# In the first two blocks the activation stays in PSUM and VectorE makes its low part; four units' attention weights are scaled on ScalarE

## Chip, cores and metric

The kernel runs on one core of one Trainium2 chip, as one program. The metric is the device time of that core in microseconds (us). Engines are named as the profile names them: PE is TensorE (PEld its weight loads), DVE is VectorE, ACT is ScalarE, POOL is GpSimd, SP is SyncE, which here issues most of the DMAs.

## What is computed

Three layers follow each other. First comes windowed attention over 4 batches of 8 heads of 576 positions (half of the heads see the last 32 positions, half every fourth of the last 128); then a dense layer; then a layer of eight experts, of which each token takes two.

```
attn = exp(scores - max);  attn = attn / (sum(attn) + 1e-9);  y = attn @ v
h = x @ w_in                      # 2304 x 512 times 512 x 2048
g = h * cos(h)
x1 = g @ w_out                    # 2304 x 2048 times 2048 x 512
top-2 of 8 experts per token;  out += weight * (relu(x1 @ w1[e]) @ w2[e])
```

All of it is fp32 in and out. Matrix products of the dense layer and the experts are made of three passes in a narrower format: each operand is split in a high part and a low part (the operand less its high part), and high x high, high x low and low x high are summed.

## The kernel before

Attention works on 16 *units* (two heads of one batch each). For a unit, `a_scores` makes the scores in PSUM and their row maxima, `a_exp` makes nine ACTIVATEs (one for each of nine pieces of 64 rows per head, with the running sums read out behind each), `a_norm` multiplies the nine pieces with the reciprocal of their sums, and `a_part` transposes the pieces (lines 507 and 510) and multiplies with v (line 527, copied out by lines 535 and 544). Units 0 to 7 take the fused exponential just told; units 0 to 3 are done in an opening ahead of the loop.

The dense layer works on blocks of 256 tokens and on pairs `p` of 0 to 7 of 256 hidden columns. A *step* is one block and one pair. The first 16 steps alternate between blocks 0 and 1 (step i is pair i // 2 of block i % 2), because in this stretch the weights of the layer arrive by DMA and are cut: each 512-column piece of a pair's weights takes three VectorE instructions (`w_bits`, lines 312 to 314), then ScalarE makes the high part (line 320) and GpSimd the low part (line 321, `w_parts`). From step 16 on the weights lie ready and block after block runs through the eight pairs.

In a step TensorE makes `ph` (`g1`, line 584). Then `post` makes h * (sin²(h/2) − 0.5), which is −h * cos(h) / 2: ScalarE rounds h / 2π to an integer (line 592), VectorE takes the remainder (line 593), ScalarE takes the sine and the square (lines 595 and 596), VectorE multiplies with `ph` (line 597), ScalarE makes the high part of g (line 600) and GpSimd the low part (line 601). Two steps later TensorE uses g (`g2`, line 611). `ph` has two buffers in PSUM, and so have r and g in SBUF: the `ph` of step i is used again in step i + 2, as soon as its readers have ended.

What stands beside a step, and where in it, is told by a table (`BESIDE`, one line for each place): pieces of weights, attention of later units, splits of x for later blocks. Each engine runs its instructions in the order in which the program is written, so what waits on an engine holds up all that stands behind it. The scaling of unit 4 stands in step 0, of unit 5 ahead of step 5, of unit 6 in step 8, of unit 7 ahead of step 12. `x_split` of block 2 (line 570) stands at the end of step 14 and in step 15, and step 16 needs it.

Of the kernel before, what the change touches and what calls it, by code (L numbers as in the profile page):

```python
# [9 lines left out]
F32 = mybir.dt.float32  # L10
# [4 lines left out]
AF = mybir.ActivationFunctionType  # L15
ALU = mybir.AluOpType
# [4 lines left out]
NB = 9  # L21
# [21 lines left out]
FUSED = 8  # L43
# [186 lines left out]
def kernel(ctx: ExitStack, tc: tile.TileContext, qT, kT, v, wm, we, wg, noise, out):  # L230
    nc = tc.nc
# [254 lines left out]
    def a_norm(u):  # L486
        s = U[u][2]
        if u in SM:
            sm = SM.pop(u)
        else:  # L490
            sm = small.tile([P, NB], F32, tag="sm", name=f"sm{u}", bufs=3)
            nc.vector.tensor_reduce(sm, s, axis=AX.X, op=ALU.add)
        nc.vector.tensor_scalar(sm, sm, 1e-9, None, op0=ALU.add)
        nc.vector.reciprocal(sm, sm)
        for i in range(0, NB, 3):
            nc.gpsimd.tensor_tensor(s[:, i:i + 3], s[:, i:i + 3],
                                    sm[:, i:i + 3, None].to_broadcast([P, 3, KW]), op=ALU.mult)
# [76 lines left out]
    def g1(blk, p, cs=range(4)):  # L574
        t, w = XHL[blk], WM[p]
        if (blk, p) not in PH:
            tag, bufs = ("acc", 4) if (blk, p) == (0, 1) else ("ph", 2)
            PH[blk, p] = psum.tile([P, 2, TB], F32, tag=tag, name=f"ph{blk}_{p}", bufs=bufs)
        ph = PH[blk, p]
        for j in range(2):  # L580
            for c in cs:
                for n, (a, x) in enumerate(PASSES):
                    o = c * 256 + j * P
                    nc.tensor.matmul(ph[:, j, :], w[:, a, o:o + P], t[:, x, c, :],  # L584
                                     start=(c == 0 and n == 0 and (j == 0 or len(cs) == 4)), stop=(c == 3 and n == 2),
                                     skip_group_check=(len(cs) < 4))
        return ph.rearrange("p a b -> p (a b)")

    def post(blk, p, ph):
        r = bpool.tile([P, 512], F32, tag="r", name=f"r{blk}_{p}", bufs=2)  # L590
        n = r.bitcast(I32)
        nc.scalar.activation(n, ph, AF.Copy, scale=1.0 / TWO_PI)  # L592
        nc.vector.scalar_tensor_tensor(r, n, -TWO_PI, ph, op0=ALU.mult, op1=ALU.add)  # L593
        yield
        nc.scalar.activation(r, r, AF.Sin, scale=0.5)  # L595
        nc.scalar.activation(r, r, AF.Square)  # L596
        nc.vector.scalar_tensor_tensor(r, r, 0.5, ph, op0=ALU.subtract, op1=ALU.mult)  # L597
        yield
        g = bpool.tile([P, 2, 512], F32R, tag="g", name=f"g{blk}_{p}", bufs=2)
        nc.scalar.activation(g[:, 0, :], r, AF.Copy)  # L600
        nc.gpsimd.tensor_tensor(g[:, 1, :], r, g[:, 0, :].bitcast(F32), op=ALU.subtract)  # L601
        G[blk, p] = g

    def g2(blk, p, ts=range(2)):
# [133 lines left out]
    def r_send(blk, t):  # L738
        si, pay = RT[blk]
        for k in range(2):  # L740
# [6 lines left out]
            if blk >= NBLK - 2:  # L747
                tc.declare_no_dep(d.ins, EARLY[0].ins, reason="expert 0's first slots are final")
            scat.append(d)


    ops.update(S=a_scores, E=a_exp, N=a_norm,
               T=lambda u, c, eng="": a_trans(u, c, eng == "a"),
               A=lambda u, g, eng="": a_av(u, g, eng == "a"),
# [17 lines left out]
    for u in range(4, FUSED):  # L772
        at_step(START[u - 4] + 2, -1, a_norm, u)
        at_step(START[u - 4] + 3, 0 if u == 4 else -1, a_part, u, 0)
    pieces = [(0, 2), (0, 3)] + [(j, k) for j in range(1, NPAIR) for k in range(4) if (j, k) > (1, 1)]
    for n, (j, k) in enumerate(pieces):
        i = n // 2
# [8 lines left out]
    for u in range(4, 16):  # L786
        i = START[u - 4]
        if i > 0:
            at_step(i, 2, a_scores, u)
        if i > 0:  # L790
            at_step(i + 1, 2, a_exp, u)
        if u >= FUSED:
            at_step(i + 2, 1, a_norm, u)
        if u >= FUSED:
            at_step(i + 3, 0, a_part, u, 0)
        at_step(i + 3, 2, a_part, u, 1)
        at_step(i + 4, 0, a_part, u, 2)
        if u + 1 < 16:
            at_step(max(i + 1, 0), 0, a_loadqk, u + 1)
            at_step(i + 4, 2, a_loadv, u + 1)  # L800
# [203 lines left out]
    for line in BESIDE.split("\n"):  # L1004
        at, *names = line.split() or ("",)
        for n in names:
            i, pos = map(int, at.split(":"))
# [4 lines left out]
    for i, (blk, p) in enumerate(steps):  # L1012
        if i == 48:
            actx.close()
            c1 = ctx.enter_context(tc.tile_pool(name="c1", bufs=1, side="right"))
        ph = g1(blk, p, range(3, 4) if i < 2 else range(4))
        run(i, -1)
        po = post(blk, p, ph)
        next(po)
        if i >= 2:  # L1020
            g2(*steps[i - 2], range(1))
        for pos in (0, 1):
            run(i, pos)
            next(po, None)
        if i >= 2:
            g2(*steps[i - 2], range(1, 2))
        run(i, 2)
# [116 lines left out]
    with tc.If(over > CAP):  # L1144
        nt = nc.values_load(nti[0:1, 1:2], min_val=NTILE, max_val=NTILE + -(-(NT - CAP) // P))
        with tc.For_i(NTILE, nt, 1) as i:
            with tc.For_i(0, NE, 1) as e:
# [23 lines left out]
                for f in range(8):  # L1171
                    ph = psum.tile([P, 512], F32, tag="ph", name=f"gp_{f}", bufs=2)
# [55 lines left out]
```

## Time and profile before

| | |
|---|---|
| median of 3 runs | 1016.55 us (1016.21 to 1018.67) |
| span of the profiled execution | 1018.6 us (the page gives no other time of that execution) |
| busy, share of the span | PE 982.1 us (96%), PEld 865.9 (85%), DVE 544.7 (53%), ACT 457.1 (45%), POOL 361.2 (35%) |
| chain that ended last, by engine | PE 76%, DVE 9%, DMA 5%, ACT 4%, issue 2%, SPq 2%, POOL 1% |

The page gives the busy share of each engine over the whole span, and the share of the chain that ended last. Both are averages over stages with different limits: the first 175 us and the rest have to be read apart, for which the trace is asked by stretches. In the rows below a time is in us from the span's start, and an instruction is named by its line, its operation and its tiles.

### The profile page before, as it was taken

What the parts mean: (1) busy time and instruction counts of PE and PEld (TensorE: products, weight loads), DVE (VectorE), ACT (ScalarE), POOL (GpSimd) and SP (SyncE); (2) the same over time, 40 slices, a digit from 0 to 9 for tenths busy, and PEclk for the clock granted to TensorE, in tenths of its full rate; (3) what the DMA queues carried; (4) which work ended last, traced back from release to release, by engine and by line L of the source; (5) the groups of instructions that cost most, each with busy time, mean ns of one, the idle gap of its engine ahead of it and who ended that gap; (6) DMA issues with size and microseconds to landing.
All of it is one profiled execution on the core that took longest, in us unless ns stands there. A gap on an engine that the chain in (4) does not pass through costs nothing.

```text
span 1018.6 us, 16790 instructions
## 1 busy us (share of the span) xinstructions
PE 982.1 (96%) x6560; PEld 865.9 (85%) x6560; DVE 544.7 (53%) x1149; ACT 457.1 (45%) x907; POOL 361.2 (35%) x470
## 2 busy tenths in 40 slices
PE   7988899999999999999999999999999999999996
PEld 5867787988898888898987889898898979898895
DVE  7699886356664645344556756344453535354321
ACT  5646665554655665555555434233241414232110
POOL 5565555233542442423333232231313232332302
PEclk9798999999999999999999999999999999999998
DMA  9963202223304110000062555453434244441201
GB/s 185 332 218 119 82 19 64 85 84 118 83 15 112 41 41 16 22 1 22 1 214 63 137 155 167 141 169 112 153 123 152 72 163 139 148 161 40 84 11 59
DMA packets 70593, 105.11 MB, mean 103 GB/s; under 512 B 31251, under 2 KB 44819, under 8 KB 70512
## 3 DMA queue, kind: packets, MB, share of 16 engines
q1 hardware_dynamic: 60528, 76.34, 25.2%
q0 software_dynamic: 9984, 27.68, 8.9%
q8 instruction: 52, 0.85, 0.4%
q14 instruction: 29, 0.24, 0.1%
HBM read 85.41 MB, written 19.59 MB: 103 GB/s over the span
## 4 chain that ended last, share of the span: by engine, by line
PE 76%; DVE 9%; DMA 5%; ACT 4%; issue 2%; SPq 2%; POOL 1%; ACTq 0%; DVEq 0%; POOLq 0%
PE pe L933 21%; PE ye L968 20%; PE ph L584 14%; PE acc L611 14%; DMA raw<-in_wm 3%; DVE cut L313 3%; PE mgx L916 2%; PE sc L452 2%; DVE cut L312 1%; PE mo L527 1%; DMA ahead<-in_v 1%; DVE r L593 1%; DVE cut L314 1%; PE mt L507 1%; ACT s L482 1%
## 5 line engine op out<-in xcount | busy, mean ns | idle before, releaser
L584 PE MATMUL ph<-xhl,wm 128*128 128x256 f32 x1728 | 228.3, 288 | 9.9 <-ACT wm L320 4.3
L584 PEld LDWEIGHTS ph<-xhl,wm 128*128 128x128 f32 x1728 | 219.9, 195 | 17.5 <-ACT wm L320 4.7
L968 PE MATMUL ye<-we,h 128*128 128x512 f32 (+1 forms) x960 | 229.5, 395 | 0.0
L611 PE MATMUL acc<-wm,g 128*128 128x512 f32 x864 | 223.1, 401 | 3.3 <-POOL g L601 1.4
L968 PEld LDWEIGHTS ye<-we,h 128*128 128x128 f32 (+1 forms) x960 | 172.8, 183 | 43.0
L611 PEld LDWEIGHTS acc<-wm,g 128*128 128x128 f32 x864 | 156.1, 190 | 35.7 <-POOL g L601 2.3
L601 POOL TENSOR_TENSOR g<-r,g 128x512 fp32r<-128x512 f32 x72 | 96.5, 1341 | 175.7 <-ACT g L600 174.8
L933 PE MATMUL pe<-xga,we 128*128 128x352 f32 x768 | 125.5, 323 | 0.0
L933 PEld LDWEIGHTS pe<-xga,we 128*128 128x128 f32 x768 | 122.6, 188 | 0.4 <-issue 0.4
L981 POOL DMA_INDIRECT out<-old,tir x35 | 35.3, 1008 | 225.6 <-DVE old L979 221.3
L935 ACT ACTIVATE h<-pe 128x256 fp32r<-128x256 f32 (+1 forms) x128 | 54.4, 425 | 123.6 <-PE pe L933 115.4
L936 DVE SCALAR_TENSOR_TENSOR h<-pe,h 128x256 fp32r<-128x256 f32 (+1 forms) x128 | 60.5, 474 | 91.4 <-ACT h L935 87.7
L979 DVE SCALAR_TENSOR_TENSOR old<-ye,wts,old 128x512 f32<-128x512 f32 (+1 forms) x35 | 26.3, 750 | 135.6 <-PE ye L968 135.6
L933 PE MATMUL pe<-xgb,we 128*128 128x256 f32 x768 | 94.8, 283 | 1.4 <-DVE h L936 1.4
L933 PEld LDWEIGHTS pe<-xgb,we 128*128 128x128 f32 x768 | 93.2, 191 | 2.1 <-DVE h L936 1.8
L593 DVE SCALAR_TENSOR_TENSOR r<-r,ph 128x512 f32<-128x512 int32 x72 | 49.2, 684 | 78.3 <-ACT r L592 77.8
L849 DVE TENSOR_TENSOR we<-wraw,we 128x512 fp32r<-128x512 f32 x128 | 88.0, 698 | 4.2 <-ACT we L848 1.7
L597 DVE SCALAR_TENSOR_TENSOR r<-r,ph 128x512 f32<-128x512 f32 x72 | 49.4, 686 | 71.4 <-ACT r L596 68.5
L848 ACT ACTIVATE we<-wraw 128x512 fp32r<-128x512 f32 x128 | 78.0, 623 | 0.0
L595 ACT ACTIVATE r<-r 128x512 f32<-128x512 f32 x72 | 45.5, 632 | 55.6 <-DVE r L593 54.8
L592 ACT ACTIVATE r<-ph 128x512 int32<-128x512 f32 x72 | 42.8, 594 | 55.5 <-PE ph L584 49.3
L600 ACT ACTIVATE g<-r 128x512 fp32r<-128x512 f32 x72 | 45.5, 631 | 44.0 <-DVE r L597 31.7
(190 smaller groups left out, 1024.3 us busy)
## 6 DMA issues: line engine op xcount, KB each, us to landing
wraw<-in_we SPq DMA_DIRECT2D x64, 512.0 KB
raw<-in_wm SPq DMA_DIRECT2D x28, 512.0 KB
vts<-in_v SPq DMA_DIRECT2D x13, 384.0 KB
x1d<-x SPq DMA_DIRECT2D x9, 512.0 KB
out<-zt SPq DMA_DIRECT2D x18, 256.0 KB
kts<-in_kT SPq DMA_DIRECT2D x13, 288.0 KB
qts<-in_qT SPq DMA_DIRECT2D x26, 144.0 KB
piece<-in_wm SPq DMA_DIRECT2D x4, 512.0 KB
```

What stands on the lines that cost most here:

```text
L584: nc.tensor.matmul(ph[:, j, :], w[:, a, o:o + P], t[:, x, c, :], start=(c == 0 and n == 0 and (j == 0 or len(cs) == 4)), stop=(c == 3 and ...
L593: nc.vector.scalar_tensor_tensor(r, n, -TWO_PI, ph, op0=ALU.mult, op1=ALU.add)
L595: nc.scalar.activation(r, r, AF.Sin, scale=0.5)
L597: nc.vector.scalar_tensor_tensor(r, r, 0.5, ph, op0=ALU.subtract, op1=ALU.mult)
L601: nc.gpsimd.tensor_tensor(g[:, 1, :], r, g[:, 0, :].bitcast(F32), op=ALU.subtract)
L611: nc.tensor.matmul(ACC[blk][t], g[:, a, j * TB + t * P:j * TB + (t + 1) * P], w[:, x, 1024 + j * DM:1024 + (j + 1) * DM], start=(p == 0 an ...
L848: nc.scalar.activation(t[:, 0, fs], raw, AF.Copy)
L849: eng.tensor_tensor(t[:, 1, fs], raw, t[:, 0, fs].bitcast(F32), op=ALU.subtract)
L933: nc.tensor.matmul(ph[:, :n], w[:, a, o:o + P], x[:, b, c, :], start=(c == 0 and i == 0), stop=(c == 3 and i == 2))
L935: nc.scalar.activation(h[:, 0, f, :], ph[:, :n], AF.Relu)
L936: nc.vector.scalar_tensor_tensor(h[:, 1, f, :], ph[:, :n], 0.0, h[:, 0, f, :].bitcast(F32), op0=ALU.max, op1=ALU.subtract)
L968: nc.tensor.matmul(acc, h[:, a, f, o:o + n], w[:, b, (f % 4) * DM:(f % 4 + 1) * DM], start=(f == 0 and i == 0), stop=(f == 7 and i == 2))
```

## The change

In `post`, for blocks 0 and 1, the product is written over `ph` in PSUM instead of over r in SBUF; the high part of g is then made from `ph`, and its low part by VectorE (from `ph` and the high part) instead of by GpSimd. In `a_norm`, for units 4 to 7, the scaling is nine ScalarE instructions, one for each piece, with the reciprocal as their scale, instead of three GpSimd instructions of three pieces each. All other blocks and units are as before.

```
@@ a_norm @@
         nc.vector.reciprocal(sm, sm)
+        if 4 <= u < FUSED:
+            for i in range(NB):
+                nc.scalar.activation(s[:, i], s[:, i], AF.Copy, scale=sm[:, i:i + 1])
+            return
         for i in range(0, NB, 3):
             nc.gpsimd.tensor_tensor(s[:, i:i + 3], s[:, i:i + 3],
                                     sm[:, i:i + 3, None].to_broadcast([P, 3, KW]), op=ALU.mult)
@@ post @@
         nc.scalar.activation(r, r, AF.Square)
-        nc.vector.scalar_tensor_tensor(r, r, 0.5, ph, op0=ALU.subtract, op1=ALU.mult)
+        v = ph if blk < 2 else r
+        nc.vector.scalar_tensor_tensor(v, r, 0.5, ph, op0=ALU.subtract, op1=ALU.mult)
         yield
         g = bpool.tile([P, 2, 512], F32R, tag="g", name=f"g{blk}_{p}", bufs=2)
-        nc.scalar.activation(g[:, 0, :], r, AF.Copy)
-        nc.gpsimd.tensor_tensor(g[:, 1, :], r, g[:, 0, :].bitcast(F32), op=ALU.subtract)
+        nc.scalar.activation(g[:, 0, :], v, AF.Copy)
+        eng = nc.vector if blk < 2 else nc.gpsimd
+        eng.tensor_tensor(g[:, 1, :], v, g[:, 0, :].bitcast(F32), op=ALU.subtract)
```

Lines shift: 592, 593, 595, 596, 597, 600 and 601 of the kernel before are 596, 597, 599, 600, 602, 605 and 607 of the changed one, and the new scaling is its line 497.

The first place is VectorE from step 8 to step 9, behind the reciprocals of unit 6 (`ph_4` and `r_4` belong to pair 4, `cut` to a piece of weights). Before:

```order
L494 RECIPROCAL sm_1262<-sm_1262 128x9
L312 TENSOR_SCALAR cut_2_1281<-raw_979 128x512
L313 SCALAR_TENSOR_TENSOR cut_2_1281<-raw_979,cut_2_1281 128x512
L314 SCALAR_TENSOR_TENSOR cut_2_1281<-raw_979,cut_2_1281 128x512
L593 SCALAR_TENSOR_TENSOR r_4_1319<-r_4_1319,ph_4_1294 128x512
L597 SCALAR_TENSOR_TENSOR r_4_1319<-r_4_1319,ph_4_1294 128x512
```

And changed:

```order
L494 RECIPROCAL sm_1274<-sm_1274 128x9
L312 TENSOR_SCALAR cut_2_1299<-raw_985 128x512
L313 SCALAR_TENSOR_TENSOR cut_2_1299<-raw_985,cut_2_1299 128x512
L314 SCALAR_TENSOR_TENSOR cut_2_1299<-raw_985,cut_2_1299 128x512
L607 TENSOR_TENSOR g_4_1303<-ph_4_1184,g_4_1303 128x512
L597 SCALAR_TENSOR_TENSOR r_4_1337<-r_4_1337,ph_4_1312 128x512
L602 SCALAR_TENSOR_TENSOR ph_4_1312<-r_4_1337,ph_4_1312 128x512
```

The low part of step 8's g now stands in VectorE's row, between the weights and the remainder of step 9.

The second place is ScalarE at the same time: the nine exponentials of unit 6, and what stands behind them up to the sine of step 9. Before:

```order
L482 ACTIVATE s_1231,sm_1262<-sc_0_1233,mx_1232 128x96 x5
L482 ACTIVATE s_1231,sm_1262<-sc_1_1242,mx_1232 128x96 x4
L320 ACTIVATE wm_1226<-cut_1_1256 128x512
L600 ACTIVATE g_4_1285<-r_4_1213 128x512
L592 ACTIVATE r_4_1319<-ph_4_1294 128x512
L595 ACT_TABLE_LOAD
L595 ACTIVATE r_4_1319<-r_4_1319 128x512
L596 ACTIVATE r_4_1319<-r_4_1319 128x512
```

And changed:

```order
L482 ACTIVATE s_1243,sm_1274<-sc_0_1245,mx_1244 128x96 x5
L482 ACTIVATE s_1243,sm_1274<-sc_1_1254,mx_1244 128x96 x4
L497 ACTIVATE s_1243<-s_1243,sm_1274 128x96 x9
L320 ACTIVATE wm_1238<-cut_1_1268 128x512
L605 ACTIVATE g_4_1303<-ph_4_1184 128x512
L596 ACTIVATE r_4_1337<-ph_4_1312 128x512
L599 ACT_TABLE_LOAD
L599 ACTIVATE r_4_1337<-r_4_1337 128x512
L600 ACTIVATE r_4_1337<-r_4_1337 128x512
```

The nine scalings stand between the exponentials and everything that step 8 and step 9 still want of ScalarE.

The third place is VectorE in step 14. Before:

```order
L597 SCALAR_TENSOR_TENSOR r_7_1696<-r_7_1696,ph_7_1671 128x512
L544 COPY xraw<-mo_0_1708 128x2x48
L544 COPY xraw<-mo_0_1708 128x2x96
L312 TENSOR_SCALAR cut_2_1736<-piece_2_1590 128x512
L313 SCALAR_TENSOR_TENSOR cut_2_1736<-piece_2_1590,cut_2_1736 128x512
```

And changed:

```order
L602 SCALAR_TENSOR_TENSOR ph_7_1720<-r_7_1720,ph_7_1695 128x512
L548 COPY xraw<-mo_0_1732 128x2x48
L548 COPY xraw<-mo_0_1732 128x2x96
L607 TENSOR_TENSOR g_7_1751<-ph_7_1695,g_7_1751 128x512
L312 TENSOR_SCALAR cut_2_1760<-piece_2_1614 128x512
L313 SCALAR_TENSOR_TENSOR cut_2_1760<-piece_2_1614,cut_2_1760 128x512
```

The low part of g stands ahead of the last two pieces of weights, and so ahead of the splits of x for step 16, which follow those.

## Rows read from the trace of the kernel before

**Rows 1.** Busy time by stretch: us, each engine's busy us (instructions), clock, DMA share, GB/s.
```profile
44.00:175.00 131.00, 113.08 (x793) 97.05 (x793) 113.41 (x153) 78.05 (x168) 73.33 (x58) 0.93 0.38 117
175.00:1018.60 843.60, 830.75 (x5417) 737.66 (x5415) 402.21 (x934) 351.77 (x623) 266.94 (x365) 1.00 0.30 94
```

**Rows 2.** Waits, 44 to 175 us: waiter, waited for, us in total, times, longest.
```profile
DVE r L597 <- ACT r L596: 8.8, 7, 1.4
```

**Rows 3.** Timeline of VectorE: start, us, line, operation, tiles.
```profile
103.23 1.65 DVE L314 SCALAR_TENSOR_TENSOR cut<-raw,cut 128x512 uint32<-128x512 uint32 x1
104.81 0.67 DVE L593 SCALAR_TENSOR_TENSOR r<-r,ph 128x512 f32<-128x512 int32 x1
105.41 0.41 DVE L312 TENSOR_SCALAR cut<-raw 128x512 uint32<-128x512 uint32 x1
...
120.43 0.69 DVE L314 SCALAR_TENSOR_TENSOR cut<-raw,cut 128x512 uint32<-128x512 uint32 x1
```

**Rows 4.** Timeline of GpSimd, the same columns; in brackets idle time and releaser.
```profile
101.31 1.34 POOL L321 TENSOR_TENSOR wm<-cut,wm 128x512 fp32r<-128x512 f32 x1 [2.02 <-ACT wm L320]
102.61 1.73 POOL L601 TENSOR_TENSOR g<-r,g 128x512 fp32r<-128x512 f32 x1
```

**Rows 5.** Timeline of VectorE: first and last beside line 601, beside line 496.
```profile
50.44 1.67 DVE L314 SCALAR_TENSOR_TENSOR cut<-raw,cut 128x512 uint32<-128x512 uint32 x1
...
165.98 1.52 DVE L312 TENSOR_SCALAR cut<-piece 128x512 uint32<-128x512 uint32 x1
...
54.44 1.04 DVE L313 SCALAR_TENSOR_TENSOR cut<-raw,cut 128x512 uint32<-128x512 uint32 x1
...
154.01 1.04 DVE L314 SCALAR_TENSOR_TENSOR cut<-piece,cut 128x512 uint32<-128x512 uint32 x1
```

**Rows 6.** Groups by line and shape, VectorE, PSUM and SBUF source: busy, mean ns, idle.
```profile
L919 DVE TENSOR_TENSOR xgb<-mgx,xgb 128x512 fp32r<-128x512 f32 x16 | 11.1, 692 | 10.0 <-ACT xgb L918 10.0
...
L570 DVE TENSOR_TENSOR xhl<-xraw,xhl 128x512 fp32r<-128x512 f32 x1 | 0.7, 683 | 0.0
```

**Rows 7.** Timeline of VectorE: first and last of four held by line 321.
```profile
74.26 1.52 DVE L312 TENSOR_SCALAR cut<-raw 128x512 uint32<-128x512 uint32 x1
...
109.18 1.36 DVE L312 TENSOR_SCALAR cut<-raw 128x512 uint32<-128x512 uint32 x1
```

**Rows 8.** Groups by line and shape, ScalarE, 44 to 175 us, columns as in rows 6.
```profile
L482 ACT ACTIVATE s<-sc,mx 128x96 f32<-128x96 f32 x27 | 8.8, 355 | 0.0
...
L569 ACT ACTIVATE xhl<-xraw 128x256 fp32r<-128x256 f32 x2 | 0.8, 404 | 0.0
```

**Rows 9.** Timeline of ScalarE, behind the exponentials of units 6 and 7.
```profile
121.38 0.38 ACT L482 ACTIVATE s<-sc,mx 128x96 f32<-128x96 f32 x1
121.60 0.25 ACT L482 ACTIVATION_READ_ACCUMULATOR s<-sc,mx 128x1 f32 x1
...
125.38 0.63 ACT L595 ACTIVATE r<-r 128x512 f32<-128x512 f32 x1 [0.70 <-DVE r L593]
...
149.02 0.38 ACT L482 ACTIVATE s<-sc,mx 128x96 f32<-128x96 f32 x1
...
164.59 0.64 ACT L600 ACTIVATE g<-r 128x512 fp32r<-128x512 f32 x1 [0.90 <-PE acc L611]
```

**Rows 10.** Timeline of VectorE: products of steps 9 and 12, last split of x.
```profile
126.70 0.69 DVE L597 SCALAR_TENSOR_TENSOR r<-r,ph 128x512 f32<-128x512 f32 x1 [1.36 <-ACT r L596]
...
154.97 0.67 DVE L597 SCALAR_TENSOR_TENSOR r<-r,ph 128x512 f32<-128x512 f32 x1
...
172.75 0.41 DVE L570 TENSOR_TENSOR xhl<-xraw,xhl 128x256 fp32r<-128x256 f32 x1
```

**Rows 11.** Timeline of TensorE: the matmuls of `ph` of step 13.
```profile
148.47 3.04 PE L584 MATMUL ph<-xhl,wm 128*128 128x256 f32 x24
```

**Rows 12.** Busy time by stretch, columns as in rows 1.
```profile
104.00:108.00 4.00, 2.18 (x16) 1.76 (x16) 3.93 (x5) 1.86 (x3) 1.67 (x2) 1.00 0.03 8
108.00:112.00 4.00, 4.00 (x33) 3.52 (x33) 3.97 (x6) 2.20 (x4) 2.69 (x2) 0.57 0.02 4
```

## Prediction

> **What bounds the kernel now.** First comes the busy time by stretch [rows 1]. Behind 175 us TensorE is busy 830.75 of 843.6 us and nothing of the change lies there, so what the change gives or costs has to be read ahead of 175 us, and a shift of that point shifts the end. From 44 to 175 us VectorE and TensorE are busy alike (113.4 and 113.1 of 131 us), so the second view is the waits of this stretch: VectorE's largest is for ScalarE's square, 8.8 us over seven times [rows 2]. So the stretch is VectorE's row, with ScalarE's chain of rounding, sine and square inside it.
>
> Third comes the timeline of VectorE, since its instructions don't cost the same every time. A free line 314 takes 0.69 us and the one at 103.23 took 1.65 [rows 3]. At that time GpSimd ran lines 321 and 601 back to back, 101.31 to 104.34, and line 314 ended 0.54 us behind line 601 [rows 4]. Line 593, which reads one operand in PSUM, took 0.67 right behind [rows 3], and none of its kind was held. So VectorE stands still while GpSimd runs, where all its operands are in SBUF. Counted over the timeline, 13 VectorE instructions are held by a line 601, together 11.5 us over their free time, and seven by a line 496, 0.35 us each, 2.45 us together; the first and the last of both are shown [rows 5].
>
> **The change, part by part.** My sum is a walk along the engines' new rows from 44 to 175 us: free durations for VectorE, a hold wherever a line 321 of GpSimd still runs beside it, and ScalarE in its new order. I give its terms and the shift (plus is later) at marks which the trace of before shows.
>
> *The low part of g.* It becomes 16 VectorE instructions with one operand in PSUM. The nearest row is the same operation with the same operands on the experts' x, 692 ns [rows 6]; the next instruction starts 0.60 us after such a start, as behind line 593 [rows 3], so 16 cost 9.6 us of the row, against 11.5 us of holds that go. The bounds: the 0.60 could be the whole 0.69 (11.1 us), or be less where VectorE would have waited anyway; the write into PSUM has no row and I take it at the price of the write into SBUF, with 0.1 us either way for each of 16.
>
> [...]
>
> There is a stall too. In steps 3, 5, 6 and 7 the low part stands right behind the product, and ScalarE's high part lies between: 0.82 us of waiting each, 3.3 us together. While VectorE waits, line 321 passes, which before held the next instruction of the weights; four such holds, together 4.1 us, go; the first and the last are shown [rows 7]. Up to step 7 that is −7.3 (eight holds by line 601) + 4.8 (eight new instructions) + 3.3 − 4.1 = −3.3 us. ScalarE's scaling of units 4 and 5 delays the remainders of steps 1 and 5, 1.6 us net of the holds by line 496. **Mark 1, the remainder of step 8: 1.7 us earlier.**
>
> *The scaling.* Nine ACTIVATEs of 96 columns with a pointer as scale. No row has just that. An exponential of the same size with a pointer takes 355 ns from PSUM [rows 8], and its follower starts 0.22 us after it [rows 9]; I take the middle, 0.29 us, 2.6 us for a unit. The bounds are 9 x 0.22 = 2.0 and, from a copy of 256 columns in SBUF, 9 x 0.404 = 3.6 us [rows 8].
>
> [...]
>
> Unit 6: before, its last exponential ended at 121.76 and the product of step 9 started at 126.70, 4.9 us later, with 0.70 us of slack ahead of the sine [rows 9, 10]. Now the chain is: reciprocals 0.5, scaling 2.6, then high part of weights, high part of g and rounding 1.7, table load 1.3, sine and square 1.35: 7.45 us. VectorE has one cut of weights to do meanwhile and then waits, since the low part of step 8 stands ahead of the remainder and needs a ScalarE instruction that is behind the scaling. That is 2.55 us more. **Mark 2, the product of step 9 (126.70): 0.8 us later.** In steps 9 to 11 three holds by line 601 (2.3 us) and one by line 321 (0.6) go against two new instructions and a stall (1.5). **Mark 3, step 11: 0.6 us earlier.**
>
> Unit 7: before, 149.40 to the product of step 12 at 154.97, 5.6 us [rows 9, 10]. Now: high parts of weights and g 1.2, low part of g and reciprocals 1.0, scaling 2.6, rounding and a high part 1.1, table load 1.3, sine and square 1.3: 8.5 us, 2.9 more. **Mark 4: 2.3 us later.** Steps 12 to 14 are a ping-pong of ScalarE and VectorE and give none of it back. In step 14 the low part of g stands ahead of the last two pieces of weights and waits for ScalarE's high part, which waits for TensorE's `acc` at 164.59 [rows 9]; before, VectorE went on without it. That costs 1.5 us, and a hold of 1.1 us by line 601, the last of the 13, goes [rows 5]. **Mark 5, the last split of x (172.75): 2.75 us later**, and step 16 on TensorE with it.
>
> *`ph` held longer.* TensorE may refill `ph` only after the low part. Step 13's matmuls began at 148.47 [rows 11]; in the walk they wait until 150.7, and step 14's until 159.3. TensorE gets to step 16 2.1 us later, so it is ahead of mark 5 and this costs nothing of its own, unless the clock falls (below).
>
> The sum is +2.75 us on 1018.6. The profiled span is 2 us above the median of the runs, within their spread, so I put the shift on the median: **1019.3 us**. About 0.3%, 3.05 us, is what a measurement can tell from no change.
>
> **Rivals.**
> *The gain survives.* If the scaling hides beside other work, what is left is 9.6 − 11.5 − 2.45 = −4.4 us, 1012.2 us. For it: ScalarE is busy only 78 of 131 us [rows 1]. Against it: behind unit 6's exponentials ScalarE has 0.70 us of slack for 2.6 us of work [rows 9]. It decides from a price of 0.13 us for a scaling, where the two units on the path lose 2.75 us less; the bound from below is 0.22.
>
> *TensorE hides it.* TensorE is as busy in the stretch as VectorE [rows 1]. If the holds that go are worth 2 us more than the walk has, marks 4 and 5 fall ahead of TensorE's own work and nothing moves: 1016.5, give or take 1.5. Against it: the last split of x, which step 16 needs, ended at 173.16 [rows 10], so VectorE is no earlier than TensorE there.
>
> [...]
>
> [...]
>
> **How the numbers follow.** The walk: 0.55, with its own range 1017.3 to 1021.0 (0.22 us of price on either side for a scaling group, 1.5 for the holds). The gain survives: 0.15, of which 0.12 is faster by over 0.3%. TensorE hides it: 0.12. The clock falls: 0.18, all slower by over 0.3%. Of the walk 0.24 lies above 1019.6. So faster 0.12, same 0.46, slower 0.42. The range 1013.3 to 1022.6 leaves out half of the gain's case and the end of the clock's.
>
> **What would show it.** Right: lines 313 and 314 with a mean nearer to 0.69 than now; nine scalings at 0.25 to 0.32 us from start to start; VectorE idle for 2 us ahead of line 607 of step 8, named as waiting for ScalarE; the last split of x near 175.5. Wrong, in the first place: scalings at 0.2 or less, or ScalarE reaching the sine of step 9 before VectorE has the remainder; and a product into PSUM that is 0.3 us longer than into SBUF would add 4 us.

## The result and the profile after

The changed kernel is slower: 1023.1 us as the median of eight runs (1019.58 to 1026.93), beside 1018.29 for the kernel before (eight runs, 1016.21 to 1019.30). The ratio is 1.0051, with an interval of 1.0037 to 1.0066, or +5.2 us (3.8 to 6.7). The forecast was +2.75 us, and 1019.3 us. Measured a second time (e9) the ratio was 1.0046 (1.0031 to 1.0062), or +4.7 us (3.2 to 6.3).

The busy time of the same two stretches as in [rows 1], now of the changed kernel:

```profile
44.00:175.00 131.00, 111.80 (x773) 97.24 (x773) 103.57 (x166) 84.90 (x200) 37.89 (x30) 0.91 0.38 116
175.00:1021.50 846.50, 833.04 (x5432) 739.98 (x5432) 404.53 (x938) 352.97 (x625) 264.43 (x364) 1.00 0.30 93
```

VectorE is busy for 10 us less than in [rows 1] although it runs more instructions: the holds by lines 601 and 496 of GpSimd are gone. ScalarE is busy for 7 us more. Still the stretch is longer, so the answer is in the waits. For 44 to 178 us (waiter, waited for, us in total, times, longest):

```profile
DVE ph L602 <- ACT r L600: 9.8, 7, 1.9
...
DVE r L597 <- ACT r L596: 8.4, 4, 3.1
...
DVE g L607 <- ACT g L605: 7.5, 9, 1.9
...
PE ph L588 <- DVE g L607: 5.7, 4, 2.6
```

Before, VectorE waited for two of ScalarE's stations, 8.8 us for the square [rows 2] and 6.0 for the rounding:

```profile
DVE r L593 <- ACT r L592: 6.0, 5, 1.8
```

Now it waits for all three (square, rounding, high part of g), up to 3.1 us at a time. The holds that went were turned into waits. The prices themselves, as groups by line from 44 to 175 us (busy, mean ns, idle before), first two lines of the kernel before:

```profile
L313 DVE SCALAR_TENSOR_TENSOR cut<-raw,cut 128x512 uint32<-128x512 uint32 x24 | 31.2, 1300 | 0.8
L314 DVE SCALAR_TENSOR_TENSOR cut<-raw,cut 128x512 uint32<-128x512 uint32 x24 | 24.4, 1016 | 0.8
```

And the changed kernel:

```profile
L313 DVE SCALAR_TENSOR_TENSOR cut<-raw,cut 128x512 uint32<-128x512 uint32 x24 | 25.7, 1072 | 0.8
...
L314 DVE SCALAR_TENSOR_TENSOR cut<-raw,cut 128x512 uint32<-128x512 uint32 x24 | 17.6, 732 | 0.8
...
L602 DVE SCALAR_TENSOR_TENSOR ph<-r,ph 128x512 f32<-128x512 f32 x15 | 10.4, 691 | 8.8 <-ACT r L600 8.8
L607 DVE TENSOR_TENSOR g<-ph,g 128x512 fp32r<-128x512 f32 x15 | 10.3, 689 | 7.6 <-ACT g L605 7.5
L497 ACT ACTIVATE s<-s,sm 128x96 f32<-128x96 f32 x36 | 10.0, 362 | 2.1 <-DVE sm L494 2.1
```

The low part from PSUM takes 689 ns, as [rows 6] had it, and the product into PSUM 691. Line 314 is nearly free now. Line 313 isn't: in the timeline ten of its instructions still take 1.1 to 1.7 us, and with a few of lines 312 and 314 VectorE is held for about 14 us over their free time, nearly always by line 321, which the change leaves on GpSimd.

**How the two traces are laid over each other.** The opening ahead of step 0 ends at a different time in every profiled execution: the remainder of step 0 starts between 39.5 and 44.8 us over the fourteen traces of this case, though the opening is the same in all of them. So a mark is counted from that remainder, in both traces. VectorE before, the remainders of steps 0, 8 and 11 (marks 2, 4 and 5 stand in [rows 10]):

```profile
44.76 0.69 DVE L593 SCALAR_TENSOR_TENSOR r<-r,ph 128x512 f32<-128x512 int32 x1 [1.77 <-ACT r L592]
...
113.22 0.68 DVE L593 SCALAR_TENSOR_TENSOR r<-r,ph 128x512 f32<-128x512 int32 x1
...
142.95 0.68 DVE L593 SCALAR_TENSOR_TENSOR r<-r,ph 128x512 f32<-128x512 int32 x1
```

And of the changed kernel, the same three with the products of steps 9 and 12 and the last split of x:

```profile
43.55 0.69 DVE L597 SCALAR_TENSOR_TENSOR r<-r,ph 128x512 f32<-128x512 int32 x1 [1.80 <-ACT r L596]
...
111.38 0.68 DVE L597 SCALAR_TENSOR_TENSOR r<-r,ph 128x512 f32<-128x512 int32 x1
...
127.19 0.70 DVE L602 SCALAR_TENSOR_TENSOR ph<-r,ph 128x512 f32<-128x512 f32 x1 [1.80 <-ACT r L600]
...
142.07 0.68 DVE L597 SCALAR_TENSOR_TENSOR r<-r,ph 128x512 f32<-128x512 int32 x1
...
157.37 0.69 DVE L602 SCALAR_TENSOR_TENSOR ph<-r,ph 128x512 f32<-128x512 f32 x1
...
175.51 0.41 DVE L574 TENSOR_TENSOR xhl<-xraw,xhl 128x256 fp32r<-128x256 f32 x1
```

Mark 5, for one: 175.51 − 43.55 = 131.96 us, against 172.75 − 44.76 = 127.99 before, is 3.97 us later. From that split to the end of the span these two traces need the same, 845.99 and 845.85 us, as the prediction had it; over all fourteen it is 844.5 to 848.1 us. All marks, in us against before (plus is later), with the time of each run:

| kernel | mark 1, step 8 | mark 2, step 9 | mark 3, step 11 | mark 4, step 12 | mark 5, split of x | ratio to before (interval) |
|---|---|---|---|---|---|---|
| predicted | −1.7 | +0.8 | −0.6 | +2.3 | +2.75 | |
| the change | −0.63 | +1.70 | +0.33 | +3.61 | +3.97 | 1.0051 (1.0037 to 1.0066) |
| e9, the change again | −0.39 | +1.92 | +0.81 | +4.09 | +4.30 | 1.0046 (1.0031 to 1.0062) |
| e1, g part alone | −3.31 | −2.66 | −4.01 | −4.13 | −1.84 | 0.9968 (0.9955 to 0.9981) |
| e2, scaling alone | +2.50 | +4.85 | +4.49 | +6.43 | +6.27 | 1.0061 (1.0047 to 1.0074) |
| e3, scaling of 4 and 5 | −0.40 | +0.22 | −1.13 | −1.30 | +1.02 | 1.0001 (0.9990 to 1.0012) |
| e4, scaling of 6 and 7 | −3.11 | −0.78 | −0.56 | +2.72 | +4.42 | 1.0025 (1.0014 to 1.0036) |
| e5, own sums | −1.56 | +0.76 | −0.60 | +2.68 | +2.88 | 1.0025 (1.0011 to 1.0040) |
| e6, g part, step 11 in SBUF | −3.12 | −2.49 | −3.84 | −3.32 | −3.13 | 0.9968 (0.9955 to 0.9981) |
| e7, g part, all in SBUF | −1.38 | −0.26 | −1.33 | −0.82 | −0.01 | 1.0003 (0.9987 to 1.0018) |
| e8, scaling on VectorE | −1.05 | +1.20 | +0.74 | +2.01 | +2.38 | 1.0042 (1.0026 to 1.0057) |
| e10, put together | −3.96 | −3.32 | −4.68 | −4.17 | −4.00 | 0.9947 (0.9932 to 0.9962) |
| e11, unit 6 scaled later | −0.43 | −1.15 | +3.20 | +6.48 | +6.69 | 1.0082 (1.0066 to 1.0099) |
| e12, scaling doubled | −0.58 | +4.13 | +3.09 | +8.77 | +10.41 | 1.0118 (1.0098 to 1.0139) |

Mark 5 and the ratio (0.001 is 1.02 us) agree to within 2 us in every row, where an interval is 1.1 to 2.1 us to either side; in e1, e4 and e8 mark 5 lies 0.1 to 0.8 us outside the interval. The marks repeat to 0.5 us between two traces of the same kernel (the change and e9), so they show what the times alone can't. Both of the change's marks lie inside its intervals, so the times fit a loss that lies wholly between step 0 and step 16, to within 2 us; the marks show where in it each part is won or lost.

### The profile page after: what moved, and what is told of

The parts are those of the page before. It is cut to its first block, busy times and chain, and to the rows that moved or that the text cites. A ratio compares the mean times of both kernels' runs of the same rounds, so it can differ in the third digit from the quotient of the medians.

```text
span 1021.5 us, 16786 instructions
## 1 busy us (share of the span) xinstructions
PE 982.8 (96%) x6560; PEld 868.2 (85%) x6560; DVE 537.5 (53%) x1165; ACT 466.1 (46%) x943; POOL 324.6 (32%) x442
## 4 chain that ended last, share of the span: by engine, by line
PE 78%; DVE 9%; ACT 6%; issue 3%; DMA 2%; SPq 1%; POOL 1%; ACTq 0%; DVEq 0%; POOLq 0%
PE pe L939 21%; PE ye L974 20%; PE ph L588 15%; PE acc L617 14%; DVE cut L313 2%; PE sc L452 2%; PE mo L531 2%; PE mgx L922 2%; PE mt L511 1%; DVE cut L312 1%; ACT s L497 1%; DMA ahead<-in_v 1%; DVE cut L314 1%; ACT s L482 1%; DVE r L597 1%
## 5 line engine op out<-in xcount | busy, mean ns | idle before, releaser
L607 POOL TENSOR_TENSOR g<-r,g 128x512 fp32r<-128x512 f32 x56 | 72.2, 1291 | 170.9 <-ACT g L605 164.5
L321 POOL TENSOR_TENSOR wm<-cut,wm 128x512 fp32r<-128x512 f32 x32 | 41.9, 1312 | 98.9 <-ACT wm L320 96.4
L602 DVE SCALAR_TENSOR_TENSOR r<-r,ph 128x512 f32<-128x512 f32 x56 | 38.4, 686 | 62.6 <-ACT r L600 59.7
```

The source lines that it names most:

```text
L607: eng.tensor_tensor(g[:, 1, :], v, g[:, 0, :].bitcast(F32), op=ALU.subtract)
```

## The experiments

**The two halves (e1, e2).** Theory S: the scaling on ScalarE is the loss, and the low part of g on VectorE is a gain. e1 leaves the scaling on GpSimd, e2 the low part of g.

```
e1:  -        if 4 <= u < FUSED:
     +        if False:
e2:  -        v = ph if blk < 2 else r
     +        v = r
     -        eng = nc.vector if blk < 2 else nc.gpsimd
     +        eng = nc.gpsimd
```

> The change's first half alone: product written into ph, low part of g on VectorE; the heads of units 4 to 7 stay on GpSimd. Theory S (the scaling on ScalarE is the whole loss, the low part of g is a gain): the time falls below before by 2 to 5 us, 0.995 to 0.998, and the last split of x comes 2 to 5 us earlier counted from the start of step 0's remainder. Rival P (ph held until the low part is done, and the low part waiting in VectorE's row, are the loss): 3 to 5 us above before, about 1.004, with step 13's and 14's matmuls still waiting 2.6 and 1.1 us for the low part. Rival T (TensorE is as late as VectorE, so a gain can't show): within 1 us of before.

> The change's other half alone: heads of units 4 to 7 scaled on ScalarE; product and low part of g as before (SBUF, GpSimd). Theory S: 6 to 10 us above before, 1.006 to 1.010, since the holds by the low part of g come back on top of the scaling. Rival P: within 1.5 us of before. Rival T: 4 to 6 us above before, as the whole change.

e1 is faster than before by 3.2 us (1.9 to 4.6), e2 slower by 6.2 us (4.8 to 7.5). Theory S holds and the rivals P and T fall: the half that holds `ph` longer is the half that gains (the last split of x 1.84 us earlier, just under the 2 expected). The two halves add up to +3.0, and the whole change was +5.2 with an interval that reaches down to 3.8; by mark 5 they add up to +4.43 against 3.97 and 4.30.

**Which units (e3, e4).** Both have the g part; e3 scales units 4 and 5 on ScalarE, e4 units 6 and 7.

```
e3:  -        if 4 <= u < FUSED:
     +        if u in (4, 5):
e4:  +        if u in (6, 7):
```

> The changed kernel, but only units 4 and 5 are scaled on ScalarE, 6 and 7 on GpSimd. Theory S with the price on units 6 and 7: 0 to 3 us below before (5 to 7 below the whole change), the product of step 9 and of step 12 no later than before. Theory S with the price on unit 5's late exponential: 1 to 2 us below the whole change only. Rival P: as the whole change, 4 to 5 us above before.

> The changed kernel, but only units 6 and 7 are scaled on ScalarE, 4 and 5 on GpSimd. Theory S with the price on units 6 and 7: 2.5 to 4.5 us above before, at most 2 us below the whole change. Theory S with the price on unit 5: within 1 us of before. Rival P: as the whole change, 4 to 5 us above before.

Against e1, at mark 1, units 4 and 5 cost 3.31 − 0.40 = 2.9 us; at mark 4, units 6 and 7 cost 4.13 + 2.72 = 6.85 us. Units 6 and 7 cost more, as the theory said, but units 4 and 5 are not free: e3 is level with before, at the upper end of what was expected. In e4 part of the 6.85 is TensorE's: it waited 2.21 us for the low part of step 8, the 24 matmuls behind took 5.49 us instead of 3.04, and ScalarE's rounding stood idle for them, which it did not in the change. With the scaling of 4 and 5 in place (the change against e3) units 6 and 7 cost 3.61 + 1.30 = 4.9 us. TensorE in e4, step 10's matmuls, with the rounding behind them, and the row of busy time around them (granted clock 0.50):

```profile
118.54 5.49 PE L588 MATMUL ph<-xhl,wm 128*128 128x256 f32 x24 [2.21 <-DVE g L607]
```

```profile
124.07 0.60 ACT L596 ACTIVATE r<-ph 128x512 int32<-128x512 f32 x1 [1.05 <-PE ph L588]
```

```profile
120.00:124.00 4.00, 4.00 (x20) 4.00 (x20) 3.01 (x5) 2.17 (x5) 0.00 (x0) 0.50 0.00 0
```

**The missing microsecond (e5).** At the remainder of step 4 the changed kernel is 0.52 us ahead of before, at that of step 5 it is 0.42 behind. ScalarE ahead of unit 5's exponentials, before:

```profile
82.24 0.63 ACT L600 ACTIVATE g<-r 128x512 fp32r<-128x512 f32 x1
82.89 1.28 ACT L482 ACT_TABLE_LOAD   x1
84.18 0.34 ACT L482 ACTIVATE s<-sc,mx 128x96 f32<-128x96 f32 x1
```

The same with the change:

```profile
80.52 0.60 ACT L605 ACTIVATE g<-ph 128x512 fp32r<-128x512 f32 x1
81.95 1.28 ACT L482 ACT_TABLE_LOAD   x1 [0.84 <-DVE mx L467]
83.25 0.34 ACT L482 ACTIVATE s<-sc,mx 128x96 f32<-128x96 f32 x1
```

Before, the table load ran while VectorE still made the row maxima; now the load itself waits for them, 0.84 us. The list of the instructions with their waits says why:

```
before:   L592 ACTIVATE r_2_887<-ph_2_858 128x512 [waits PE_49,Pool_49]
          L482 ACT_TABLE_LOAD
          L482 ACTIVATE s_909,sm_967<-sc_0_911,mx_910 128x96 [waits DVE_49]
changed:  L596 ACTIVATE r_2_893<-ph_2_864 128x512 [waits PE_49]
          L482 ACT_TABLE_LOAD [waits DVE_49]
          L482 ACTIVATE s_915,sm_973<-sc_0_917,mx_916 128x96 [waits Pool_49]
```

The sums of unit 5's exponentials go into one of three buffers (`sm`), whose last reader was GpSimd's scaling of an earlier unit. Before, ScalarE's rounding in the steps ahead waited for GpSimd too (r came free with line 601), and that covered the buffer as well. With line 601 gone from these blocks the rounding waits for TensorE alone, and the exponential has two waits of its own; one of them now stands on the load ahead of it. So the wait belongs to the low part of g and not to the scaling: it is in e1's trace as well, and not in e2's. First e1, then e2:

```profile
79.21 1.28 ACT L482 ACT_TABLE_LOAD   x1 [0.84 <-DVE mx L467]
```

```profile
84.57 1.28 ACT L482 ACT_TABLE_LOAD   x1
```

e5 gives these sums a buffer that GpSimd never read:

```
-        sm = small.tile([P, NB], F32, tag="sm", name=f"sm{u}", bufs=3)
+        tag, bufs = ("sm5", 1) if u == 5 else ("sm", 3)
+        sm = small.tile([P, NB], F32, tag=tag, name=f"sm{u}", bufs=bufs)
```

> The changed kernel; only the sums of unit 5's exponentials get a buffer of their own, so that the exponential no longer has to wait for GpSimd and VectorE both. Theory W (the 0.84 us ahead of unit 5's table load comes from a wait that the load has to carry because the exponential has two): the load follows the high part of g at once, the remainder of step 5 and all marks behind it come 0.8 to 0.9 us earlier counted from step 0's remainder, the last split of x 3.1 us later than before instead of 3.96, the time 0.5 to 1.3 us below the whole change. Rival L (the held line 467 itself is late, whoever waits): the exponentials start at most 0.3 us earlier and the marks stay.

ScalarE in e5 (the high part of g is line 606 there, the exponential 483):

```profile
77.95 0.60 ACT L606 ACTIVATE g<-ph 128x512 fp32r<-128x512 f32 x1
78.57 1.28 ACT L483 ACT_TABLE_LOAD   x1
79.86 0.34 ACT L483 ACTIVATE s<-sc,mx 128x96 f32<-128x96 f32 x1
```

The load follows at once, though VectorE's line 467 was held as long as before (0.86 us at 78.45), and all marks behind it come 0.93 to 1.09 us earlier. That is shown, and rival L falls. With this one wait gone, the marks are −1.56, +0.76, −0.60, +2.68 and +2.88: the prediction's walk, to 0.4 us at each. The ratio fell from 1.0046 and 1.0051 to 1.0025, more than the 0.5 to 1.3 us expected, but between measurements on different chips.

**What became of e1's gain (e6).** e1 was 4.13 us ahead at mark 4 and only 1.84 at mark 5. In step 13 TensorE waits for the low part of step 11, since `ph` has two buffers. e6 writes that one product into SBUF.

```
-        v = ph if blk < 2 else r
+        v = ph if blk < 2 and (blk, p) != (1, 5) else r
```

> The g part alone (as e1), but step 11's product goes into SBUF, so that its ph comes free 2.5 us earlier, for step 13's matmuls. Theory C (in e1 the 2 us lost behind step 12 are TensorE's: 2.66 us of waiting for the low part of step 11, and the lower clock behind it): step 13's 24 matmuls start at once behind step 11's and take 3.0 to 3.4 us instead of 4.34, the last split of x comes 3.5 to 4.2 us earlier than before counted from step 0's remainder (e1: 1.85), the time 1 to 2.5 us below e1. Rival A (the loss is ScalarE's and VectorE's alternation in steps 12 to 14): the marks within 0.5 us of e1.

Step 13's matmuls on TensorE, first in e1 (with its row of busy time, granted clock 0.73), then in e6:

```profile
145.28 4.34 PE L588 MATMUL ph<-xhl,wm 128*128 128x256 f32 x24 [2.66 <-DVE g L607]
```

```profile
148.00:152.00 4.00, 4.00 (x21) 3.62 (x21) 2.81 (x4) 2.16 (x5) 3.32 (x3) 0.73 0.46 127
```

```profile
142.29 3.04 PE L588 MATMUL ph<-xhl,wm 128*128 128x256 f32 x24
```

Without the wait they take 3.04 us, at a granted clock of 1.00 (140 to 148 us), and from mark 4 to mark 5 e6 loses 0.19 us where e1 loses 2.29. Theory C holds for the mechanism. Its sum was too high: the low part of step 11, now with all operands in SBUF, took 1.37 us instead of 0.69, with GpSimd busy for 2.95 us of 144 to 148, and that is most of the 0.8 by which mark 4 is later than in e1. The net 1.3 us of the marks doesn't show in the times: e1 and e6 have the same ratio, and the expected 1 to 2.5 us below e1 were not seen.

e1's row at 0.73 lies behind 2.66 us of idle time; e6, without the gap, has 1.00 in that stretch too. Not every gap was followed by slower matmuls: in e4 step 13's took 3.14 us behind a wait of 2.66.

**Does the place of the product matter (e7)?** As e1, but all 16 products in SBUF, low part on VectorE.

```
-        v = ph if blk < 2 else r
+        v = r
```

> The low part of g on VectorE as in e1, but the product stays in SBUF for all 16 steps, so that line 607 has no operand in PSUM; ph comes free at the product. Theory H (an instruction of VectorE with all operands in SBUF stands still while GpSimd runs): some of the 16 take 1 to 1.7 us instead of 0.69, step 8's remainder comes 1 to 3 us later than in e1 (there 3.3 earlier than before), and steps 13 and 14 lose nothing to the wait for ph; in all 1 us below to 2 us above e1. Rival N (the place of the product is of no weight to VectorE): all 16 at 0.69, marks up to step 11 as in e1, and about 2 us below e1 at the end.

The low parts as a group by line, e1 and then e7:

```profile
L607 DVE TENSOR_TENSOR g<-ph,g 128x512 fp32r<-128x512 f32 x16 | 11.0, 689 | 6.4 <-ACT g L605 6.3
```

```profile
L607 DVE TENSOR_TENSOR g<-r,g 128x512 fp32r<-128x512 f32 x16 | 15.0, 935 | 6.3 <-ACT g L605 6.3
```

With both operands in SBUF the mean is 935 ns, eight of the 16 taking 0.94 to 1.58 us; with one in PSUM none takes more than 0.69. Mark 1 is 1.9 us later than in e1, and the gain over before is gone (1.0003; against e1 1.8 us by mark 5 and 3.6 by the times, where up to 2 was expected). Theory H holds: the low part on VectorE pays because its operand lies in PSUM.

**Another engine for the scaling (e8).** The change, with VectorE for the multiplication of units 4 to 7 (three instructions of 288 columns a unit).

```
-            for i in range(NB):
-                nc.scalar.activation(s[:, i], s[:, i], AF.Copy, scale=sm[:, i:i + 1])
-            return
+            eng = nc.vector
+        else:
+            eng = nc.gpsimd
         for i in range(0, NB, 3):
-            nc.gpsimd.tensor_tensor(s[:, i:i + 3], s[:, i:i + 3],
+            eng.tensor_tensor(s[:, i:i + 3], s[:, i:i + 3],
         ...
```

> The changed kernel with the heads of units 4 to 7 scaled by VectorE, three multiplications of 288 columns a unit in place of ScalarE's nine. Theory S (the loss is the nine ScalarE instructions between the exponentials and the rounding and sine that VectorE waits for): 3 x 0.45 us a unit, 5.4 us at most in VectorE's row against 2.45 us of holds by GpSimd's three that go; 0 to 3 us above e1, that is 1013 to 1017 if before is at 1016.7, and 5 us below the whole change. Rival D (whatever engine scales ahead of the transposes, the delay is the same): within 1.5 us of the whole change.

Theory S's number was missed: e8 is 4.3 us above before, 1.6 (by mark 5) ahead of the change and 4.2 behind e1. The three instructions of unit 5 took 2.27 us, not 1.35, and those of the other units 2.12 to 2.27:

```profile
84.00 2.27 DVE L500 TENSOR_TENSOR s<-s,sm 128x288 f32<-128x288 f32 x3
```

The median of the twelve is 0.45 us, but the longest takes 1.52. That line 321 holds the long ones is an inference from the change, where line 313 took 1.64 us at 87.04, beside line 321 at 86.86. By that, on VectorE the scaling is held by GpSimd, and on ScalarE it holds up VectorE: the price is nearly the same. By the times (1.0042 against 1.0046 and 1.0051) rival D's number came, but e1 speaks against its reason: with the scaling at the same place on GpSimd the delay isn't there.

**Another place for the scaling (e11).** Unit 6's scaling behind step 9's high part of g, its first transposes in step 10.

```
-8:1 ... a_exp(6) a_norm(6) w_parts(5,1) ...
+8:1 ... a_exp(6) w_parts(5,1) ...
-9:2 a_part(6,0)
-10:0 w_parts(5,2)
+9:2 a_norm(6)
+10:0 a_part(6,0) w_parts(5,2)
```

> The changed kernel with unit 6's scaling moved on ScalarE from ahead of the rounding and sine of step 9 to behind step 9's high part of g, and the first transposes of unit 6 behind the next rounding. Theory S (it costs because VectorE waits for the chain it stands in): the product of step 9 comes 2.2 to 2.6 us earlier than in the changed kernel; step 10's rounding is then 1.0 to 1.5 late, and 0.7 to 1.4 us are left at step 11 and at the last split of x. Rival B (ScalarE's 2.5 us are on the path wherever they stand): step 10's remainder as in the changed kernel, within 0.3.

The product of step 9 came 2.85 us earlier than in the change (2.2 to 2.6 expected), and then all was lost and more: mark 3 is 2.9 us later than in the change, the ratio 1.0082. TensorE in e11 waits for the scaling and for the copies behind the transposes, and its next matmuls run at a granted clock of 0.50:

```profile
124.11 1.78 PE L511 MATMUL mt<-ident,s 128*96 128x128 f32 x6 [1.69 <-ACT s L497]
127.09 1.28 PE L531 MATMUL mo<-at,vts 96*64 96x64 f32 x20 [1.20 <-ACT at L514]
...
128.82 2.91 PE L617 MATMUL acc<-wm,g 128*128 128x512 f32 x6
```

```profile
128.00:132.00 4.00, 4.00 (x20) 3.33 (x19) 1.29 (x3) 2.20 (x5) 2.55 (x2) 0.50 0.01 4
```

The six matmuls into `acc` take 2.91 us; six at 139.28 in the same trace take 1.63. Rival B was nearer, but it too expected no more than the same. TensorE's two waits, 2.9 us together, read as VectorE's 2.5 us in another place; since the edit moves the scaling and the transposes at once, e11 alone doesn't tell their parts.

**The price doubled (e12).** A second pass of nine scalings by a constant one, for units 6 and 7.

```
+            for i in range(NB if u >= 6 else 0):
+                nc.scalar.activation(s[:, i], s[:, i], AF.Copy, scale=nc.const_aps.tensor(1.0, [P, 1], F32))
```

> The changed kernel with a second pass of nine scalings by one behind the first, for units 6 and 7 alone (a doubled cost; the numbers are the same). Theory S: both units are on the path, each pass of 2.5 us costs 2.5 at the product of step 9 and 2.5 more at that of step 12: the last split of x 4.5 to 5.2 us later than in the changed kernel, the time 4 to 5.5 above it. Rival Q (part of the price of units 6 and 7 is the lower clock or the wait for ph, not the instructions): under 3.5 us.

A pass costs 2.43 us at mark 2 and 2.73 more at mark 4 (8.77 − 3.61 = 5.16 for the two), so the nine instructions are on the path with their full 2.5 us in both places. From mark 4 to mark 5 it loses 1.64 us where the change loses 0.36, which theory S didn't have: step 14's matmuls now wait 3.47 us for the low part and then take 4.57 us, against 3.14 in the change:

```profile
163.08 4.57 PE L590 MATMUL ph<-xhl,wm 128*128 128x256 f32 x24 [3.47 <-DVE g L609]
```

So the whole was more than theory S expected: the last split of x is 6.4 us later than in the change (4.5 to 5.2 expected), and the time 7.3 us above it (4 to 5.5), by e9, which ran beside it.

**Put together (e10).** From e1, e5 and e6: low part of g on VectorE from PSUM, step 11's from SBUF, scaling on GpSimd, unit 5's sums in their own buffer. Its edits are those shown.

> A version put together from the runs: low part of g on VectorE with the product in ph, but step 11's product in SBUF; heads scaled by GpSimd as before; unit 5's sums in a buffer of their own. If the three pieces add, the last split of x comes 3.14 + 0.9 = 4.0 us earlier than before counted from step 0's remainder, and the time is 3.5 to 4.5 us below before (about 0.996). If TensorE now is the later of the two, no more than the 3.1 of e6.

The marks add as expected: the last split of x is 4.00 us earlier than before. The time is 1011.18 us against 1016.60 for before and 1021.83 for the change, run beside it; the ratio to before, 0.9947 (0.9932 to 0.9962), is −5.4 us (3.9 to 6.9), where 3.5 to 4.5 were expected. ScalarE ahead of unit 5 in e10, with the load at once, and the last split of x (39.46 was its step 0):

```profile
74.64 0.60 ACT L606 ACTIVATE g<-ph 128x512 fp32r<-128x512 f32 x1
75.27 1.28 ACT L483 ACT_TABLE_LOAD   x1
```

```profile
163.45 0.41 DVE L575 TENSOR_TENSOR xhl<-xraw,xhl 128x256 fp32r<-128x256 f32 x1
```

**The change again (e9).**

> The changed kernel once more, unaltered, beside before on this chip. If the marks tell the time, it is 3.5 to 4.5 us above before (the last split of x came 3.96 later, counted from step 0's remainder), and the first measurement's 4.8 was 0.8 of scatter. If something outside the stretch from step 0 to step 16 costs too, it is 4.8 to 5.5 again. The marks agree with the first trace within 0.15 us.

The marks came out 0.2 to 0.5 us later than in the first trace, more than the 0.15 expected, and the ratio is again above mark 5, by 0.4 us (the first time by 1.2). Both 3.97 and 4.30 lie inside the intervals, so the rest isn't shown to be anything but scatter; it stays open.

## Why the prediction was wrong

The direction was right, and so was the mechanism, but for one wait that the walk has no term for; the size was not: +2.75 forecast, about +4 by the marks, +4.7 and +5.2 by the times.

- **The step that failed** is mark 1, "the remainder of step 8: 1.7 us earlier", which came 0.63 earlier; all marks behind it are 0.9 to 1.3 us later than forecast. Two things in it were wrong. The walk has no term for the wait on unit 5's table load: it let the load follow the high part of g, as in the kernel before. e5 puts that wait at 0.93 us, and it comes with the low part of g (e1 has it, e2 has not). And the term "ScalarE's scaling of units 4 and 5 delays the remainders of steps 1 and 5, 1.6 us net" was too small: it measured 2.4 us without the wait (e5 against e10) and 2.7 with it (the change against e1). At the remainder of step 4, ahead of unit 5, the change is already 1.97 us behind e1, so most of it is unit 4's; how the 1.6 was divided between the two isn't on record, and why it was too small stays open. The low part of g brought 3.96 us at mark 1 (e10), 0.7 more than forecast, which by luck covers the 0.8 that the scaling costs more. So e5, with the wait taken away, has the marks of the walk, to 0.13 us at mark 5.
- **The base.** The shift was put on the median of three runs, 1016.55 us. Beside the changed kernel the kernel before had 1018.29, beside the experiments 1016.6 to 1017.4. So of the 3.8 us between 1019.3 and 1023.1, 1.7 are the base and 2.1 the shift.
- **The low part of g** was right in sign and nearly in size. Up to step 7 the term was −3.3 us; mark 1 is at −3.31 in e1, but with the wait on the load in it, so that the two meet is luck; without the wait it is −3.96 (e10). The prices were right too: 689 ns from PSUM, the write into PSUM at 691 against 683 ns. The product 0.3 us longer, which would have cost 4 us, did not come.
- **The scaling of units 6 and 7** was right in price and in effect. Nine take 2.50 us, inside the bounds, against 2.6 forecast:

```profile
120.56 2.51 ACT L497 ACTIVATE s<-s,sm 128x96 f32<-128x96 f32 x9 [0.55 <-DVE sm L494]
122.97 0.61 ACT L320 ACTIVATE wm<-cut 128x512 fp32r<-128x512 f32 x1
123.49 0.57 ACT L605 ACTIVATE g<-ph 128x512 fp32r<-128x512 f32 x1
123.97 0.58 ACT L596 ACTIVATE r<-ph 128x512 int32<-128x512 f32 x1
124.56 1.28 ACT L599 ACT_TABLE_LOAD   x1
125.86 0.63 ACT L599 ACTIVATE r<-r 128x512 f32<-128x512 f32 x1
```

  This is the chain of unit 6 that the prediction wrote down, in its order. From mark 1 to mark 2 it cost 2.33 us (2.5 forecast), and from mark 3 to mark 4 unit 7 cost 3.28 (2.9 forecast). VectorE stood idle for 1.89 us ahead of step 8's low part, named as waiting for ScalarE; 2 us were forecast.
- **`ph` held longer** was right for this kernel. Step 13's matmuls wait until 150.39, step 14's until 159.53. Counted from step 0's remainder, which is 1.21 us earlier in this trace than in that of before, they are 0.9 and 1.4 us later than the 150.7 and 159.3 forecast, as late as marks 3 and 4 are. For the same reason the last split of x at 175.51 does not bear out "near 175.5": by the count it is 1.2 us later than forecast.

```profile
150.39 4.61 PE L588 MATMUL ph<-xhl,wm 128*128 128x256 f32 x24 [2.64 <-DVE g L607]
...
159.53 3.14 PE L588 MATMUL ph<-xhl,wm 128*128 128x256 f32 x24 [1.10 <-DVE g L607]
```

  The first wait was followed by a granted clock of 0.67 (152 to 156 us) and matmuls of 4.61 us instead of 3.04, and yet step 14 still had 1.10 us to wait for VectorE, so TensorE was not the later of the two. A falling clock, of which [rows 12] show one, had 0.18 of the chances and the upper end of the range; no run shows that it adds to the shift of the whole change: from mark 4 to mark 5, behind this gap, the change loses 0.36 us (0.45 in the walk, without a fall). Here the slower matmuls cost nothing that shows, while in e1, e4, e11 and e12, where TensorE was nearer to being late, they did.
- **The rivals.** "The gain survives" needed scalings at 0.13 us; they take 0.28. "TensorE hides it" is refuted by e1: a gain ahead of step 16 reaches the end.

## What to carry to other kernels

When an instruction is moved off an engine, list the waits of what stays, not only the order: a wait that it caused may have covered others, which then turn up somewhere worse, here on a table load that had been free. Before handing work to an engine that looks idle, ask what stands behind it in that engine's row: 2.5 us between the exponentials and the next rounding were 2.5 us of the kernel, twice, though ScalarE was busy for 60% of the time. Compare two traces from a common start behind the opening, and a gain in one stage can be measured to half a microsecond where the times of one kernel scatter by two to eight.

## What the runs showed of the hardware

- The table load ahead of unit 5's exponentials, which in the change carries a wait for VectorE, stood idle until that was met: 0.84 us ahead of it in the change, none in e5, with the same maxima at the same place.
- The same subtraction on VectorE took 0.68 to 0.69 us each time (mean 689 ns) with one operand in PSUM (e1) and 0.68 to 1.58 us (mean 935 ns) with both in SBUF (e7).
- Behind waits of TensorE for the low part of g (2.64 us in the change, 2.66 in e1, 2.21 in e4, 3.47 in e12) the 24 matmuls of a step took 4.61, 4.34, 5.49 and 4.57 us instead of 3.04, with a granted clock of 0.67 in the change (152 to 156 us), 0.73 in e1 (148 to 152) and 0.50 in e4 (120 to 124); behind another wait of 2.66 us in e4 they took 3.14. So the price of these gaps of TensorE was not their length alone: in e1 2.66 us of waiting for `ph` and 1.3 us of slower matmuls turned a lead of 4.1 us into 1.8.
